# A third buffer for a transposed operand in a fused window-attention training kernel, paid for by loading weights twice

## Chip, cores and metric

The kernel runs on one core of one Trainium2 chip. The metric is the device time of one execution in microseconds; the time before is 1979.6 us, the median of three runs (1979.23 to 1980.32). Single executions of this kernel scatter by up to about 1.5%, and not every chip gives the same median, so each comparison below names the runs of the kernel before that were made beside it on the same chip. Chips are called by the numbers in the records of the runs; that of the first result isn't recorded.

In the text, TensorE does the matrix products, ScalarE is ACT in the profile, VectorE is DVE, GpSimd is POOL, and SyncE is SP, which here does nothing but issue transfers.

## The reference

The forward pass of attention in 8x8 windows of a 256x256 image with 384 channels, and its gradients for the input and for both weight matrices, all in bfloat16:

```python
B, H, W, C = x.shape                     # 1, 256, 256, 384
win = 8
xw  = windows(x)                         # [1024 windows, 64 tokens, C]
qkv = xw @ wqkv
q, k, v = qkv[..., :C], qkv[..., C:2*C], qkv[..., 2*C:]
p = softmax(einsum('bqc,bkc->bqk', q, k) * C**-0.5)
o = einsum('bqk,bkc->bqc', p, v) @ wo
out = image(o)
# reference(x, wqkv, wo, grad_out): out and the vjp's gradients of x, wqkv and wo
```

(The two reshapes between image and windows are abbreviated as `windows` and `image`.)

## The kernel before

The kernel multiplies the weight matrices with each other at the start, so that each window needs only two projections: y from the input (X) and h from the output gradient (DO). It works in 128 steps of 8 windows (512 tokens; the code calls such a unit a quad). Within step n, TensorE does the attention products of quad n, the scores of quad n+2 and the projections of quad n+3. The parts that matter here:

```python
NX, ND, NXT, NDT, NYH, NTOK, NVW = 13, 5, 3, 2, 2, 2, 9
...
YHT = sb.tile([P, NYH, 2, CK, 512], BF16, name="YHT")      # y and h, channels on the partitions
YH = sb.tile([P, NTOK, 2, CK * 4, P], BF16, name="YH")     # the same, tokens on the partitions
w_sb = sb.tile([P, CK, J], BF16, name="w_sb")              # the weights, kept to the end

def load_do(q, n):
    for t in range(4):
        q.dma_start(out=DO[:, (n % ND) * 4 + t, :], in_=img(grad_out, n, t))

def turn_yh(n, a):                                         # a transposing transfer, issued by SyncE
    SP.dma_start_transpose(out=YH[:, n % NTOK, a, :, :],
                           in_=YHT[:, n % NYH, a, :, :].rearrange("p m t -> p (m t)"))

def proj(n, a, banks, engs):
    ...                                                    # TensorE into a PSUM bank, then
            ev(engs[i], YHT[:, n % NYH, a, mo, P * t0:P * t1], o)      # the bank is copied to YHT

def chain3(n):                                             # softmax, last part
    ...
    DVE.tensor_reduce(out=ST[:, 3, :], in_=TM[:], axis=AX.X, op=ALU.add)
    POOL.tensor_tensor(out=UM[:], in0=pb[:, 1], in1=bcast(3), op=ALU.mult)
    POOL.tensor_tensor(out=pb[:, 0], in0=TM[:], in1=UM[:], op=ALU.subtract)

def step(n):
    S, A = n + 2, n + 3
    turn_in(n + 4, 0)                      # transposes of X and of DO, also on SyncE
    turn_in(n + 4, 1)
    md(n)                                  # the step's first matrix products
    ...                                    # attention of n, which reads YH[n % NTOK]
    load_do(SP, n + 5)                     # four loads on SyncE
    turn_yh(S, 0)
    turn_yh(S, 1)                          # writes YH[S % NTOK] from YHT[S % NYH]
    ...
    proj(A, 0, ...)                        # overwrites YHT[A % NYH]
    outs(n, ...)
    proj(A, 1, ...)
```

In one step SyncE thus has eight transfers to issue in a fixed order: two transposes of the inputs, four loads of DO, and the pair of YH transposes, which this document calls the YH pair.

Of the kernel before, what the change touches and what calls it, by code (L numbers as in the profile page):

```python
# [9 lines left out]
ALU = mybir.AluOpType  # L10
AX = mybir.AxisListType
BF16 = mybir.dt.bfloat16
# [4 lines left out]
def kernel(  # L17
# [12 lines left out]
    _, H, W, C = x.shape  # L30
    P = 128
    CK = C // P
    J = 3 * C
    JK = J // P
    NQC = W // 32
    NQ = (H // 16) * NQC
    scale = float(C) ** -0.5
    GQ = 6
    NX, ND, NXT, NDT, NYH, NTOK, NVW = 13, 5, 3, 2, 2, 2, 9

    def cut(q):

        out = []
        while q + GQ <= NQ - 2:
            out.append(tuple(range(q, q + GQ)))
            q += GQ
        if q < NQ - 2:
            out.append(tuple(range(q, NQ - 2)))
        return out + [(q,) for q in range(NQ - 2, NQ)]

    groups = [cut(0), [tuple(range(GQ // 2))] + cut(GQ // 2)]
    PE, DVE, ACT, POOL, SP = nc.tensor, nc.vector, nc.scalar, nc.gpsimd, nc.sync

    sb = ctx.enter_context(tc.tile_pool(name="sb", bufs=1))
    pp = ctx.enter_context(tc.tile_pool(name="pp", bufs=1, space=bass.MemoryType.PSUM))
    PS = pp.tile([P, 8, 512], F32, name="PS")
# [3 lines left out]
    XT = sb.tile([P, NXT, 4 * CK, P], BF16, name="XT")  # L60
# [12 lines left out]
    TM = sb.tile([P, 4, 64], F32, name="TM")  # L73
    UM = sb.tile([P, 4, 64], F32, name="UM")
    ST = sb.tile([P, 4, 4], F32, name="ST")
    ACC = sb.tile([P, 2 * CK, C], F32, name="ACC")
    ident = sb.tile([P, P], BF16, name="ident")
    w_sb = sb.tile([P, CK, J], BF16, name="w_sb")
    A_sb = sb.tile([P, CK, C], BF16, name="A_sb")
    AT_sb = sb.tile([P, CK, C], BF16, name="AT_sb")  # L80
    B_sb = sb.tile([P, CK, C], BF16, name="B_sb")
# [16 lines left out]
    def bcast(col):  # L98
        return ST[:, col, :].unsqueeze(2).to_broadcast([P, 4, 64])
# [10 lines left out]
    def turn_in(n, a):  # L110
        src = (X[:, (n % NX) * 4:(n % NX) * 4 + 4, :] if a == 0 else DO[:, (n % ND) * 4:(n % ND) * 4 + 4, :])
        SP.dma_start_transpose(out=XT[:, n % NXT, :, :] if a == 0 else DOT[:, n % NDT, :, :],
                               in_=src.rearrange("p t c -> p (t c)"))
# [35 lines left out]
    def sd(r, w):  # L149
        return PS[HALF[r], 4, w * 256:w * 256 + 256].rearrange("p (t k) -> p t k", t=4)  # L150
# [11 lines left out]
    def chain3(n):  # L162
        pb = PB[:, n % 2]
        DVE.tensor_reduce(out=ST[:, 1, :], in_=PEX[:], axis=AX.X, op=ALU.add)
        DVE.reciprocal(out=ST[:, 2, :], in_=ST[:, 1, :])
        DVE.tensor_tensor(out=pb[:, 1], in0=PEX[:], in1=bcast(2), op=ALU.mult)  # L166
        for w in range(2):
            DVE.tensor_tensor(out=TM[HALF[w]], in0=sd(1 - w, w), in1=pb[HALF[w], 1], op=ALU.mult)  # L168
        DVE.tensor_reduce(out=ST[:, 3, :], in_=TM[:], axis=AX.X, op=ALU.add)
        POOL.tensor_tensor(out=UM[:], in0=pb[:, 1], in1=bcast(3), op=ALU.mult)  # L170
        POOL.tensor_tensor(out=pb[:, 0], in0=TM[:], in1=UM[:], op=ALU.subtract)

    def turn_p(n):
        bb = PS[:, 7, 256:512].bitcast(BF16)
        for t in range(4):
            for a in range(2):
                for w in range(2):
                    r = slice(64 * w, 64 * w + 64)
                    o = t * P + a * 64
                    PE.transpose(bb[r, o:o + 64], PB[r, n % 2, a, t, :], ident[r, r])  # L180
        DVE.tensor_copy(out=TT[:, n % 2, :, :, :].rearrange("p t a k -> p (t a k)"), in_=bb)
# [98 lines left out]
    class Block:  # L280
# [25 lines left out]
        def add(self, bank):  # L306
            self.banks -= 1
            dst = GF if self.last and self.banks == 0 else ACC
            if self.adds:
# [24 lines left out]
    flat = VW[:].rearrange("p a b c -> p (a b c)")  # L334
    wT = flat[:, 0:JK * C].rearrange("p (j c) -> p j c", j=JK)
    wo_sb = flat[:, JK * C:(JK + CK) * C].rearrange("p (m c) -> p m c", m=CK)
    GF = YHT[:, 0].rearrange("p a m t -> p (a m t)")[:, 0:6 * C].rearrange("p (k c) -> p k c", k=6)
    GFT = YHT[:, 1].rearrange("p a m t -> p (a m t)")[:, 0:6 * C].rearrange("p (k c) -> p k c", k=6)
    bank = [0]
# [12 lines left out]
    def step(n):  # L352
        S, A = n + 2, n + 3
        doS, doA = S < NQ, A < NQ
        early = not todo
        if n + 4 < NQ:
            turn_in(n + 4, 0)
            turn_in(n + 4, 1)

        md(n)  # L360
        if early:
            if doA:
                proj(A, 0, (3, 4, 0, 5), (ACT, ACT, ACT, DVE))
            if n + 1 < NQ:
                turn_p(n + 1)
            attn_vw(n, 0, 0)
            vw_ev(n, 0, 0, ACT)
            attn_vw(n, 1, 2 * 512)
            attn_vw(n, 2, 2 * 512 + 2 * C)
            vw_ev(n, 1, 2 * 512, DVE)  # L370
            vw_ev(n, 2, 2 * 512 + 2 * C, ACT)
            attn_vw(n, 3, 0)
            vw_ev(n, 3, 0, ACT)
            if doS:
                stack(S, 0, 0, 3)
                stack(S, 1, 0, 3)
            if n + 5 < NQ:
                load_x(POOL, n + 5)
        else:
            blk = todo.pop(0)  # L380
            nb = len(blk.tiles)
            i1, i2 = (7, 15) if nb == 4 * GQ else (nb // 2, nb)
            blk.mms((3, 4), 0, i1)
            attn2(n, 0, (ACT, ACT))
            if doS:
                stack(S, 0, 0, 3)
            if n + 1 < NQ:
                turn_p(n + 1)
            if doS:
                stack(S, 1, 0, 3)  # L390
            blk.mms((3, 4), i1, i2)
            blk.add(4)
            if n + 5 < NQ:
                load_x(POOL, n + 5)
            attn2(n, 1, (ACT, DVE))
        ready(n)
        if n + 5 < NQ:
            load_do(SP, n + 5)
        if doS:
            turn_yh(S, 0)  # L400
            turn_yh(S, 1)

        dxs(n, 0)
        dxs(n, 1)
        if not early:
            if doS:
                scores(S)
                chain0(S)
            dxs_ev(n, 0, ACT)
            blk.mms((3,), i2, nb)  # L410
        dxs(n, 3)
        dxs(n, 2)
        if early:
            dxs_ev(n, 0, ACT)
            if doS:
                scores(S)
                chain0(S)
        if doS:
            chain2(S)
        dxs_ev(n, 1, ACT)  # L420
        if doS:
            chain3(S)
        if not early:
            blk.add(3)
        if doA:
            proj(A, int(early), (0, 1, 2), (ACT, ACT, ACT))
        else:
            fill(0, 1, 2)
        outs(n, 0, (5, 6), ACT)
        outs(n, 2, (4, 7) if early else (0, 1), ACT)  # L430
        outs_st(n)
        if not early and doA:
            proj(A, 1, (7, 2, 4, 3), (ACT, ACT, ACT, DVE))
        elif not doA:
            fill(7, 2, 4)
# [4 lines left out]
    with tc.manual_schedule():  # L440
# [68 lines left out]
        proj(2, 1, (6, 7, 0, 4), (ACT, ACT, ACT, ACT))  # L509
        for n in range(NQ):  # L510
            step(n)
            if n == 4:
                for m in range(CK):
                    SP.dma_start_transpose(out=woT_sb[:, :, m * P:(m + 1) * P], in_=wo[m * P:(m + 1) * P, :])
# [7 lines left out]
        def ep(o, lt, rr, dst, eng, sc):  # L522
            for mb in range(CK):
                mm(o, lt(mb), rr(mb), mb == 0, mb == CK - 1)
            if eng is ACT:
                ACT.activation(out=dst, in_=o, func=ACTF.Copy, scale=scale if sc else 1.0)  # L526
            elif sc:
                DVE.tensor_scalar(out=dst, in0=o, scalar1=scale, scalar2=None, op0=ALU.mult)
            else:
                DVE.tensor_copy(out=dst, in_=o)  # L530

        def tr(h):
            for mb in range(CK):
                pt = PS[:, h * CK + mb, :].bitcast(BF16)
                for ma in range(CK):
                    PE.transpose(pt[:, ma * P:(ma + 1) * P], GF[:, h * CK + ma, mb * P:(mb + 1) * P], ident[:])
                ev(DVE if mb % 2 == 0 else ACT, GFT[:, h * CK + mb, :], pt[:, 0:C])
# [3 lines left out]
        cut = lambda ma: slice(ma * P, (ma + 1) * P)  # L541
        tr(0)
        for ma in range(CK):
            ep(PS[:, 6 + ma % 2, 0:C], lambda mb: GF[:, mb, cut(ma)], lambda mb: w_sb[:, mb, C:2 * C],
               dw[:, ma, 0:C], DVE if ma == 1 else ACT, True)
        tr(1)
        for ma in range(CK):
            ep(PS[:, ma, 0:C], lambda mb: GFT[:, mb, cut(ma)], lambda mb: w_sb[:, mb, 0:C],
               dw[:, ma, C:2 * C], DVE if ma == 0 else ACT, True)
        SP.dma_start(out=out_2.rearrange("(m p) j -> p m j", p=P)[:, :, 0:2 * C], in_=dw[:, :, 0:2 * C])  # L550
        for ma in range(CK):
            ep(PS[:, 6 + ma % 2, 0:C], lambda mb: w_sb[:, mb, 2 * C + ma * P:2 * C + (ma + 1) * P],
               lambda mb: GF[:, CK + mb, :], dwo[:, ma, :], DVE if ma == 1 else ACT, False)
        ACT.dma_start(out=out_3.rearrange("(m p) n -> p m n", p=P), in_=dwo[:])
        for ma in range(CK):
# [33 lines left out]
```

## Time and profile before

| | before |
|---|---|
| median of runs | 1979.6 us |
| span of the profiled run | 1983.8 us |
| TensorE busy | 1944.9 us, 98% |
| DMA engines, mean busy share in the middle | 1.18 (packet times, which overlap) |
| clean step of TensorE | 14.87 us |
| mean of 109 steps in the middle | 15.12 us |
| ScalarE's wait for the YH transposes | 60.9 us, 64 times |

The prediction below shows and reads the lines. Three things help to read them. A wait `A <- B` is the idle time of A that ended when B ended, with the total, the number of times and the longest. The chain is the work that ended last, followed backwards, so a wait only costs time to the extent that it, or what follows from it, is on the chain. And a queue of transfers has two times: the one in which the issuing engine is held, and the one until the data has landed.

### The profile page before, as it was taken

How to read it: one execution, taken by the hardware profiler on the slowest of the kernel's cores; microseconds unless marked ns; L12 is line 12 of the kernel's file. 1: busy time of each engine (PE TensorE's matmuls, PEld its weight loads, DVE VectorE, ACT ScalarE, POOL GpSimd, SP SyncE). 2: the span in 40 equal slices, each digit the busy share in tenths (PEclk: the TensorE clock that was granted, in tenths of full speed). 3: DMA queues.
4: the chain of work that ended last, by engine and by line, in shares of the span. 5: the costliest groups of instructions: out<-in, count | busy, mean ns of one | idle time of the engine just before them, and what ended most of it. 6: DMA issues, size and time to landing. Idle time of an engine off the chain costs nothing.

```text
span 1983.8 us, 78482 instructions
## 1 busy us (share of the span) xinstructions
PE 1944.9 (98%) x32789; PEld 1364.7 (69%) x32789; DVE 1254.8 (63%) x2595; ACT 1337.1 (67%) x2204; POOL 1317.0 (66%) x2315
## 2 busy tenths in 40 slices
PE   8899999999999999999999999999999999999999
PEld 5566776677667666767766776676677677666766
DVE  5665666666666666666666666666666666656664
ACT  5766766666666676667666766766776766667664
POOL 4766766666666667667667666666766766667653
PEclk9999999999999999999999999999999999999999
DMA  9999999999999999999999999999999999999992
GB/s 215 208 204 212 219 208 207 216 208 200 212 214 212 210 200 210 216 209 216 216 212 210 222 212 196 222 206 210 207 224 205 211 208 218 205 199 222 217 165 68
DMA packets 972260, 409.24 MB, mean 206 GB/s; under 512 B 855296, under 2 KB 947264, under 8 KB 971904
## 3 DMA queue, kind: packets, MB, share of 16 engines
q1 hardware_dynamic: 871632, 251.17, 83.5%
q0 software_dynamic: 98496, 151.78, 30.0%
q8 instruction: 256, 4.19, 0.9%
q10 hardware_dynamic: 1776, 1.28, 0.2%
q14 instruction: 100, 0.82, 0.1%
HBM read 101.84 MB, written 101.84 MB: 103 GB/s over the span
## 4 chain that ended last, share of the span: by engine, by line
PE 85%; DMA 10%; ACT 2%; DVE 1%; issue 1%; POOL 0%; ACTq 0%; DVEq 0%; POOLq 0%
PE PS L86 84%; DMA YH<-YHT 10%; PE PS L180 1%; ACT YHT L90 1%; DMA out_dram<-OS 0%; ACT VW L90 0%; DMA X<-in_x_dram 0%; DVE TM L168 0%; POOL out_dram L278 0%; DVE SS L156 0%; DVE ST L154 0%; ACT DXS L90 0%; ACT VW L526 0%; ACT OS L90 0%; DVE PB L166 0%
## 5 line engine op out<-in xcount | busy, mean ns | idle before, releaser
L278 POOL DMA_DIRECT2D out_dram<-DXS x1024 | 578.0, 571 | 570.5 <-ACT DXS L90 512.2
L86 PE MATMUL PS<-VW,X 64*64 64x384 bf16 (+1 forms) x8661 | 578.1, 325 | 0.0
L86 PEld LDWEIGHTS <-X 64*64 64x64 bf16 (+1 forms) x14805 | 445.2, 106 | 129.0 <-issue 33.6
L86 PEld LDWEIGHTS <-MD 128*128 128x128 bf16 x3840 | 343.1, 98 | 226.2 <-issue 43.2
L90 ACT CAST YHT<-PS 128x512 bf16<-128x512 f32 (+1 forms) x770 | 392.6, 556 | 91.9 <-DMA YH<-YHT 60.9
L90 ACT CAST VW<-PS 128x768 bf16<-128x768 f32 x384 | 294.2, 800 | 141.1 <-PE PS L86 141.0
L104 POOL DMA_DIRECT2D X<-in_x_dram x508 | 289.3, 581 | 25.3 <-PE PS L86 14.2
L220 POOL DMA_DIRECT2D out_dram<-OS x512 | 277.5, 549 | 26.5 <-issue 10.2
L86 PE MATMUL PS<-AT_sb,MD 128*128 128x384 bf16 (+2 forms) x2304 | 294.3, 273 | 0.5 <-ACT DXS L90 0.4
L92 DVE CAST YHT<-PS 128x256 bf16<-128x256 f32 (+1 forms) x129 | 55.2, 429 | 378.2 <-PE PS L86 369.0
L86 PE MATMUL PS<-B_sb,MD 128*128 128x384 bf16 x1536 | 274.1, 326 | 12.5 <-ACT YHT L90 7.8
L86 PE MATMUL PS<-XT,A_sb 128*128 128x512 bf16 (+1 forms) x1170 | 270.3, 376 | 2.6 <-DVE TM L168 1.9
L86 PE MATMUL PS<-DOT,BT_sb 128*128 128x256 bf16 (+1 forms) x1527 | 270.5, 327 | 0.0
L90 ACT CAST DXS<-PS 128x768 bf16<-128x768 f32 x256 | 204.2, 798 | 85.7 <-PE PS L86 75.9
L92 DVE CAST MD<-PS 128x512 bf16<-128x512 f32 x384 | 241.7, 683 | 10.7 <-PE PS L86 10.3
L90 ACT CAST OS<-PS 128x768 bf16<-128x768 f32 x256 | 202.9, 809 | 51.3 <-PE PS L86 45.1
L86 PEld LDWEIGHTS <-BT_sb 128*128 128x128 bf16 x1527 | 149.1, 98 | 112.5
L90 ACT CAST MD<-PS 128x512 bf16<-128x512 f32 x384 | 201.2, 602 | 28.2 <-PE PS L86 27.8
L86 PE MATMUL PS<-YH,PB 64*64 64x256 bf16 (+2 forms) x3072 | 211.7, 270 | 0.0
L160 ACT ACTIVATE PEX<-SS 128x256 f32<-128x256 f32 x128 | 53.3, 417 | 227.9 <-DVE SS L156 227.9
L86 PEld LDWEIGHTS <-PB 64*64 64x64 bf16 x6144 | 192.6, 107 | 16.4 <-issue 2.5
L86 PEld LDWEIGHTS <-A_sb 128*128 128x128 bf16 x1170 | 109.0, 98 | 110.3 <-issue 3.9
(65 smaller groups left out, 1938.6 us busy)
## 6 DMA issues: line engine op xcount, KB each, us to landing
out_dram<-DXS POOLq DMA_DIRECT2D x1024, 48.0 KB
out_dram<-OS POOLq DMA_DIRECT2D x512, 96.0 KB
X<-in_x_dram POOLq DMA_DIRECT2D x508, 96.0 KB
DO<-in_grad_out_dram SPq DMA_DIRECT2D x504, 96.0 KB, 5.1
YH<-YHT SPq DMA_TRANSPOSE x256, 8.2
XT<-X SPq DMA_TRANSPOSE x126, 7.4
DOT<-DO SPq DMA_TRANSPOSE x126, 8.2
DO<-in_grad_out_dram POOLq DMA_DIRECT2D x8, 96.0 KB
```

Source lines behind the costliest of these rows:

```text
L86: PE.matmul(out, lhsT=lhsT, rhs=rhs, start=start, stop=stop, skip_group_check=True)
L90: ACT.copy(out=out, in_=in_)
L92: DVE.tensor_copy(out=out, in_=in_)
L104: q.dma_start(out=X[:, (n % NX) * 4 + t, :], in_=img(x, n, t))
L160: ACT.activation(out=PEX[:], in_=SS[:], func=ACTF.Exp)
L180: PE.transpose(bb[r, o:o + 64], PB[r, n % 2, a, t, :], ident[r, r])
L220: POOL.dma_start(out=img(out_0, n, t), in_=OS[:, n % 2, t, :])
L278: POOL.dma_start(out=img(out_1, n, t)[8 * w:8 * w + 8], in_=DXS[64 * (1 - w):64 * (1 - w) + 64, n % 2, t, :])
```

## The change

The kernel gets a third slot for YHT, so that a projection's result doesn't have to overwrite data whose transpose may not have ended. The room comes from the weights: they are no longer kept (`w_sb` now lies over a buffer that is used later) but loaded a second time shortly before the end, into a buffer that is then free. Apart from that, two elementwise products at the end of the softmax go from GpSimd to VectorE.

```diff
--- before.py
+++ after.py
@@ -36,7 +36,7 @@
     NQ = (H // 16) * NQC
     scale = float(C) ** -0.5
     GQ = 6
-    NX, ND, NXT, NDT, NYH, NTOK, NVW = 13, 5, 3, 2, 2, 2, 9
+    NX, ND, NXT, NDT, NYH, NTOK, NVW = 13, 5, 3, 2, 3, 2, 9
 
     def cut(q):
 
@@ -75,7 +75,6 @@
     ST = sb.tile([P, 4, 4], F32, name="ST")
     ACC = sb.tile([P, 2 * CK, C], F32, name="ACC")
     ident = sb.tile([P, P], BF16, name="ident")
-    w_sb = sb.tile([P, CK, J], BF16, name="w_sb")
     A_sb = sb.tile([P, CK, C], BF16, name="A_sb")
     AT_sb = sb.tile([P, CK, C], BF16, name="AT_sb")
     B_sb = sb.tile([P, CK, C], BF16, name="B_sb")
@@ -167,8 +166,8 @@
         for w in range(2):
             DVE.tensor_tensor(out=TM[HALF[w]], in0=sd(1 - w, w), in1=pb[HALF[w], 1], op=ALU.mult)
         DVE.tensor_reduce(out=ST[:, 3, :], in_=TM[:], axis=AX.X, op=ALU.add)
-        POOL.tensor_tensor(out=UM[:], in0=pb[:, 1], in1=bcast(3), op=ALU.mult)
-        POOL.tensor_tensor(out=pb[:, 0], in0=TM[:], in1=UM[:], op=ALU.subtract)
+        DVE.tensor_tensor(out=UM[:], in0=pb[:, 1], in1=bcast(3), op=ALU.mult)
+        DVE.tensor_tensor(out=pb[:, 0], in0=TM[:], in1=UM[:], op=ALU.subtract)
 
     def turn_p(n):
         bb = PS[:, 7, 256:512].bitcast(BF16)
@@ -334,6 +333,8 @@
     flat = VW[:].rearrange("p a b c -> p (a b c)")
     wT = flat[:, 0:JK * C].rearrange("p (j c) -> p j c", j=JK)
     wo_sb = flat[:, JK * C:(JK + CK) * C].rearrange("p (m c) -> p m c", m=CK)
+    w_sb = flat[:, (JK + CK) * C:(JK + CK) * C + CK * J].rearrange("p (m j) -> p m j", m=CK)
+    w_end = XT[:].rearrange("p n j k -> p (n j k)")[:, 0:CK * J].rearrange("p (m j) -> p m j", m=CK)
     GF = YHT[:, 0].rearrange("p a m t -> p (a m t)")[:, 0:6 * C].rearrange("p (k c) -> p k c", k=6)
     GFT = YHT[:, 1].rearrange("p a m t -> p (a m t)")[:, 0:6 * C].rearrange("p (k c) -> p k c", k=6)
     bank = [0]
@@ -509,6 +510,8 @@
         proj(2, 1, (6, 7, 0, 4), (ACT, ACT, ACT, ACT))
         for n in range(NQ):
             step(n)
+            if n == NQ - 3:
+                SP.dma_start(out=w_end[:], in_=wqkv.rearrange("(m p) j -> p m j", p=P))
             if n == 4:
                 for m in range(CK):
                     SP.dma_start_transpose(out=woT_sb[:, :, m * P:(m + 1) * P], in_=wo[m * P:(m + 1) * P, :])
@@ -541,15 +544,15 @@
         cut = lambda ma: slice(ma * P, (ma + 1) * P)
         tr(0)
         for ma in range(CK):
-            ep(PS[:, 6 + ma % 2, 0:C], lambda mb: GF[:, mb, cut(ma)], lambda mb: w_sb[:, mb, C:2 * C],
+            ep(PS[:, 6 + ma % 2, 0:C], lambda mb: GF[:, mb, cut(ma)], lambda mb: w_end[:, mb, C:2 * C],
                dw[:, ma, 0:C], DVE if ma == 1 else ACT, True)
         tr(1)
         for ma in range(CK):
-            ep(PS[:, ma, 0:C], lambda mb: GFT[:, mb, cut(ma)], lambda mb: w_sb[:, mb, 0:C],
+            ep(PS[:, ma, 0:C], lambda mb: GFT[:, mb, cut(ma)], lambda mb: w_end[:, mb, 0:C],
                dw[:, ma, C:2 * C], DVE if ma == 0 else ACT, True)
         SP.dma_start(out=out_2.rearrange("(m p) j -> p m j", p=P)[:, :, 0:2 * C], in_=dw[:, :, 0:2 * C])
         for ma in range(CK):
-            ep(PS[:, 6 + ma % 2, 0:C], lambda mb: w_sb[:, mb, 2 * C + ma * P:2 * C + (ma + 1) * P],
+            ep(PS[:, 6 + ma % 2, 0:C], lambda mb: w_end[:, mb, 2 * C + ma * P:2 * C + (ma + 1) * P],
                lambda mb: GF[:, CK + mb, :], dwo[:, ma, :], DVE if ma == 1 else ACT, False)
         ACT.dma_start(out=out_3.rearrange("(m p) n -> p m n", p=P), in_=dwo[:])
         for ma in range(CK):
```

## The prediction

> **What bounds the kernel now.** I read the page's busy table first, then the chain of waits, then the waits summed by pair, then the two tiles that the change touches, and last the synchronising engine's own record, because the chain pointed at it.
>
> ```profile
> PE 1944.9 (98%) x32789; PEld 1364.7 (69%) x32789; DVE 1254.8 (63%) x2595; ACT 1337.1 (67%) x2204; POOL 1317.0 (66%) x2315
> DMA  9999999999999999999999999999999999999992
> PEclk9999999999999999999999999999999999999999
> PE 85%; DMA 10%; ACT 2%; DVE 1%; issue 1%; POOL 0%; ACTq 0%; DVEq 0%; POOLq 0%
> ```
>
> TensorE works 98% of the span at the full clock. At most 1983.8 - 1944.9 = 39 us of visible idle time can be won from it, 2% of the span. But the DMA row is as full as the PE row, and the chain passes through a DMA for a tenth of the span, always YH<-YHT. The chain in order of time shows how long a step of TensorE is when nothing holds it:
>
> ```profile
> 943.83 0.18 PE PS L180 x11
> 944.01 0.01 PE PS L86
> 944.02 0.07 PE PS L180 x4
> 944.08 14.62 PE PS L86 x226
> ...
> 1228.74 10.45 DMA YH<-YHT
> 1239.19 0.02 issue
> ...
> 1239.27 0.59 ACT YHT L90
> ```
>
> One clean step is 14.62 + 0.18 + 0.01 + 0.07 = 14.88 us (14.87 between the starts of most steps). The lower lines are a disturbed one: the transposing transfer of YHT lands at 1239.19, only then may ScalarE overwrite that YHT slot, and TensorE, out of PSUM banks, waits for ScalarE. Summed by pair:
>
> ```profile
> ACT YHT L90 <- DMA YH<-YHT: 60.9, 64, 3.3
> PE PS L86 <- ACT YHT L90: 18.7, 31, 1.9
> POOL UM L170 <- DVE ST L169: 12.5, 2, 6.8
> PEld L180 <- POOL PB L171: 1.2, 1, 1.2
> PE PS L180 <- POOL PB L171: 1.0, 1, 1.0
> ```
>
> This is the wait that a third slot takes away. Its whole cost is more than 18.7 us. The view by windows gives the middle of the run as a whole:
>
> ```profile
> 184.25:1832.74 1648.49, 1631.82 (x27905) 1150.86 (x27904) 1054.31 (x2180) 1128.99 (x1856) 1119.39 (x1963) 1.00 1.18 211
> 120.38:184.25 63.87, 60.48 (x1025) 42.76 (x1024) 38.77 (x80) 40.24 (x68) 45.66 (x79) 1.00 1.17 204
> 1907.00:1940.00 33.00, 33.00 (x537) 23.22 (x536) 19.79 (x41) 18.36 (x30) 16.63 (x31) 1.00 0.60 112
> ```
>
> The first stretch holds 109 steps (218 YH transposes are issued in it, two a step): 15.124 us a step, 0.254 over the clean step, 27.7 us in all. The second holds four steps, 63.87 - 4 x 14.87 = 4.4 us. So 32 us is lost to waits in the steady part: the ceiling of what the slots can return. The third stretch, near the end, shows the DMA load once input loads have stopped (share 0.60, against 1.18).
>
> Now the question is why the transfer is late. The tile view of the transposes' line, first in the middle stretch, then in 1907 to 1932:
>
> ```profile
> L116 SPq EVENT_SEMAPHORE  x327: 17/17/28, 187.4 to 1822.6; - x164
> L116 SPq DMA_TRANSPOSE YH<-YHT x218: 1544/2800/5858, 187.5 to 1822.7; - x109
> DMA to landing us min/median/max: 5.3/8.2/12.7
> ...
> L116 SPq DMA_TRANSPOSE YH<-YHT x4: 1424/1560/1681, 1911.6 to 1928.1; - x4
> DMA to landing us min/median/max: 3.8/5.1/6.0
> ```
>
> The reader is to see two things. In 109 steps no semaphore instruction ahead of these transposes lasted over 28 ns: the queue of SyncE never waits for the other engines, it is always behind. And a transpose holds the queue for 2.8 us under load, 1.56 us without. The other transposes have medians of 2.70 and 2.90 us, the four loads of a step 0.60 us each: 2 x 2.80 + 2.70 + 2.90 + 4 x 0.60 = 13.6 us, and with the small instructions between them a full step. In order of time it issues the YH pair 2.3 us after the start of the next step (913.77 against 911.43), while near the end, without load, it is 4.5 us into its own step. It runs about 12 us late.
>
> **What the Trainium skill says.** "Perfetto Trace Analysis", section "What 'DMA-bound' means", names as one of the kinds a queue whose sequencer track is solid DMA slices. This trace agrees: no pause over 28 ns at that line. The same page, section "DMA Instruction — HWDGE (DVE, Sync)", says that the reported window opens when all semaphores are satisfied; so the 2.8 us are descriptor work[...] and not a wait on an engine, which fits that it falls to 1.56 us near the end. "SBUF — State Buffer", section "Who interferes with whom", says that a two-input tensor operation in SBUF contends only with GpSimd instructions that read SBUF; after the change POOL has no such instruction in the loop. No row before can confirm that. "GPSIMD Engine Reference", section "Elementwise — side-by-side cycle accounting", gives GpSimd about twice the time of VectorE; here it is 625 and 725 ns against 424 ns for a 128x256 multiplication on VectorE, so 1.5 to 1.7.
>
> **The change part by part.**
> (1) Third YHT slot. The evacuation of projection n+3 now overwrites what was transposed a whole step earlier. The next need of the same transfer is TensorE's read of YH. In a clean step the first y cast starts 10.2 us in (906.60 against 896.39), the first h cast 13.9 us in; the first YH matmul 1.8 us into the following step, the h one about 2.2. So y may land 14.87 + 1.8 - 10.2 = 6.5 us later than now, h 14.87 + 2.2 - 13.9 = 3.2 us later. The room is thus about 3 us, not a step: NTOK stays 2, and the queue may only become 3 us later still.
> (2) Products on VectorE: minus (625 + 725) ns x 128 = 173 us of POOL (to about 1144), plus 2 x 0.424 x 128 = 109 us of VectorE (to about 1364, 69%). In a step VectorE is idle 2.99 us ahead of its YHT cast, after these products, so 0.85 us fits. It takes PB out from behind POOL's descriptor work, worth the 1.0 us of the one late wait. In the prologue the copies to HYS follow the products on VectorE and lie on the chain: plus 0.85 us once.
> (3) The weights again: 3 x 128 x 1152 x 2 bytes = 0.885 MB. At the mean 206 GB/s that is 4.3 us, issued after step 125, about 1940, where the DMA share is low and the first reader is at 1973. Nothing on the path. The first load only moves to another place.
> Sum outside the steady part: about +1 us. Inside: between -3 and -32.
>
> **The rivals.**
> A, only slots were missing: the lateness is a scatter of some 2 us that 3 us swallow. For it: most steps are clean, in runs of up to ten; waits come in bursts. Then nearly all goes: -28, 1952 us.
> B, the queue sets the pace: it never waits, and averages 15.12 us a step against 14.87. Then a deeper buffer lets it fall 3 us further behind, once, and the wait comes back as TensorE waiting for YH itself. For it: the 28 ns. Then 1979.6 + 1 - 3 = 1978 us.
> C, in between: the queue in clean steps averages nearer 15.03 (my estimate from the starts of the pair in 68 clean steps, uncertain by 0.12), and disturbed steps make the transfers bunch. Removing most waits then gains (15.12 - 15.03) x 115 = 10 us and the 3 us of room: 1968 us.
> D, VectorE becomes late with the PSUM bank 3 addition and holds the last projection: 0.85 of about 1.5 us of slack. A loss of at most some tenths a step in bad steps; I give it little.
>
> **Range and chances.** I weigh B 0.45, C 0.30, A 0.25: 0.45 x 3 + 0.30 x 13 + 0.25 x 28 = 12 us, less 1 us of the prologue: 1968.5, and I say 1968 us. Eight in ten: 1951 to 1980. Two per cent would be 39.6 us, more than the 32 us that waits take, so faster by over 2% has 0.02; slower by over 2% needs a new wait of 0.3 us in every step, 0.02; within 2% 0.96.
>
> **What would show it.** The pair ScalarE YHT waiting for YH<-YHT must be near zero; if it isn't, the reading of the slots is wrong. If A holds, TensorE's wait total falls by 19 us and nearly all steps are 14.87. If B holds, TensorE or its weight loads wait for the DMA YH<-YHT, a pair that is absent now, and the middle stretch stays near 15.1 a step. SyncE's semaphore instructions stay at 28 ns under B and C. VectorE near 1364 us, POOL near 1144. What would make it wrong: a transpose that holds the queue for another time than 2.8 us because POOL's transfers come at other moments, up or down; 0.2 us on each of four would be 100 us a run up to the floor of TensorE.

## The result

The changed kernel takes 1957.57 us (median of four runs: 1956.62, 1964.61, 1958.46, 1956.68), the kernel before 1979.96 us (median of four: 1979.6, 1979.23, 1980.32, 1988.91). The ratio is 0.9884, with a 95% interval from 0.9848 to 0.9921: 1.2% less time, which is inside 2%. A ratio in this document is the mean time of the one kernel's fast runs over the mean time of the other's fast runs of the same rounds, so it isn't quite the ratio of the medians quoted. Executions over 1.5% slower than the fastest of the same kernel are left out of the means.

The page of the changed kernel, busy times, DMA row and chain:

```profile
PE 1934.0 (99%) x32789; PEld 1350.2 (69%) x32789; DVE 1362.9 (70%) x2851; ACT 1352.0 (69%) x2204; POOL 1135.4 (58%) x2059
DMA  9999999999999999999999999999999999999992
PE 97%; DVE 1%; ACT 1%; issue 0%; DMA 0%; ACTq 0%; DVEq 0%
```

TensorE now makes up 97% of the chain (it was 85%), and the DMA, 10% before, has gone from it. Yet the DMA row is as full as it was. TensorE's waits, summed by pair (from the longest down):

```profile
PE PS L85 <- DVE TM L167: 4.3, 5, 1.8
...
PE PS L85 <- ACT YHT L89: 0.3, 1, 0.3
```

The line numbers are one lower than before, because a line was removed above; L85 is the L86 of before. The wait for ScalarE's YHT has fallen from 18.7 us to 0.3, and ScalarE's own wait for YH<-YHT, 60.9 us before, is not in the list any more. In its place there is nothing: TensorE doesn't wait for YH itself either. The windows view of the middle, 109 steps, and of four early steps (columns as in the prediction's lines of this view: window, length, busy time of PE, PEld, DVE, ACT and POOL, clock, DMA share, GB/s):

```profile
180.68:1803.67 1622.99, 1622.22 (x27905) 1137.48 (x27904) 1146.80 (x2398) 1142.13 (x1855) 966.15 (x1747) 1.00 1.18 214
121.19:180.68 59.49, 59.49 (x1025) 41.73 (x1025) 42.17 (x88) 41.99 (x70) 37.67 (x68) 1.00 1.17 216
```

1622.99 / 109 = 14.89 us a step, against 15.12 before, and 59.49 / 4 = 14.87 against 15.97. Both stretches are TensorE without a gap, and the DMA engines, at the same share, moved 214 GB/s in place of 211. The chain in order of time has TensorE alone for whole steps on end; one with a rare gap of 0.35 us, the largest exception in the 60 us that I read:

```profile
928.04 7.27 PE PS L85 x102
935.31 0.35 issue
935.66 7.51 PE PS L85 x124
```

I also took the start of every step from the trace. Over steps 6 to 124 the profiled run of before spends 31.9 us more than 119 clean steps would take, that of after 2.1 us. That difference, 29.8 us, is the whole of the difference between the two spans (29.1 us), less the 0.8 us that after loses before step 6 begins. The profiled run of before was one of its longer runs, so by the medians the gain is 22.4 us.

The moved products, as groups of the page by form, first before, then after:

```profile
L171 POOL TENSOR_TENSOR PB<-TM,UM 128x256 bf16<-128x256 f32 x128 | 93.2, 728 | 10.0
L170 POOL TENSOR_TENSOR UM<-PB,ST 128x256 f32<-128x256 bf16 x128 | 80.2, 627 | 14.5 <-DVE ST L169 12.5
```

```profile
L170 DVE TENSOR_TENSOR PB<-TM,UM 128x256 bf16<-128x256 f32 x128 | 54.4, 425 | 4.4
L169 DVE TENSOR_TENSOR UM<-PB,ST 128x256 f32<-128x256 bf16 x128 | 54.3, 424 | 4.4
```

And the queue of SyncE. First the timeline of before over one round of its eight transfers (start, time held, what), then that of after:

```profile
898.93 6.06 SPq L116 DMA_TRANSPOSE YH<-YHT  x2
905.21 2.74 SPq L112 DMA_TRANSPOSE XT<-X  x1
908.17 2.90 SPq L112 DMA_TRANSPOSE DOT<-DO  x1
911.13 2.54 SPq L108 DMA_DIRECT2D DO<-in_grad_out_dram  x4
913.77 6.88 SPq L116 DMA_TRANSPOSE YH<-YHT  x2
```

```profile
1166.90 5.26 SPq L115 DMA_TRANSPOSE YH<-YHT  x2
1172.39 2.32 SPq L111 DMA_TRANSPOSE XT<-X  x1
1174.93 2.46 SPq L111 DMA_TRANSPOSE DOT<-DO  x1
1177.44 3.02 SPq L107 DMA_DIRECT2D DO<-in_grad_out_dram  x4
1180.57 6.05 SPq L115 DMA_TRANSPOSE YH<-YHT  x2
```

In both kernels a row ends where the next begins, but for 0.05 to 0.25 us: the queue is without a pause, in after too. Over all steps, its transfer instructions hold it for 14.0 us of a step in the median in both kernels (the middle half of the steps lies between 13.9 and 14.2), and the rest is small instructions; the pauses of over 0.15 us add up to 4.9 us over the middle steps, in each of the two. (The view of SyncE's own waits doesn't show this: it lists 625.4 us of waits for TensorE ahead of L112 before, and 606.3 us at the same line after.) Its pace, from one YH pair to the same pair a step later, averages 15.12 us over the middle steps before, and 14.86 us after. That is the surprise: the queue that "sets the pace" is without a pause in both kernels, and runs faster in the one with a third slot.

### The profile page after: what moved, and what is told of

The parts are those of the page before. It is cut to its first block, busy times and chain, and to the rows that moved or that the text cites. A ratio compares the mean times of both kernels' runs of the same rounds, so it can differ in the third digit from the quotient of the medians.

```text
span 1954.7 us, 78332 instructions
## 1 busy us (share of the span) xinstructions
PE 1934.0 (99%) x32789; PEld 1350.2 (69%) x32789; DVE 1362.9 (70%) x2851; ACT 1352.0 (69%) x2204; POOL 1135.4 (58%) x2059
## 2 busy tenths in 40 slices
DMA packets 972659, 410.12 MB, mean 210 GB/s; under 512 B 855312, under 2 KB 947280, under 8 KB 972304
## 4 chain that ended last, share of the span: by engine, by line
PE 97%; DVE 1%; ACT 1%; issue 0%; DMA 0%; ACTq 0%; DVEq 0%
PE PS L85 95%; PE PS L179 2%; ACT VW L89 0%; DVE TM L167 0%; DMA X<-in_x_dram 0%; ACT YHT L89 0%; DVE SS L155 0%; DVE ST L153 0%; ACT DXS L89 0%; ACT VW L529 0%; ACT OS L89 0%; DVE PB L165 0%; DVE ST L163 0%; PE PS L187 0%; ACTq L103 0%
## 5 line engine op out<-in xcount | busy, mean ns | idle before, releaser
L85 PE MATMUL PS<-VW,X 64*64 64x384 bf16 (+1 forms) x8661 | 574.6, 324 | 0.0
L85 PEld LDWEIGHTS <-X 64*64 64x64 bf16 (+1 forms) x14805 | 435.1, 106 | 121.0 <-issue 22.6
L85 PEld LDWEIGHTS <-MD 128*128 128x128 bf16 x3840 | 343.3, 98 | 215.5 <-issue 31.7
L89 ACT CAST YHT<-PS 128x512 bf16<-128x512 f32 (+1 forms) x770 | 409.2, 553 | 16.5 <-PE PS L85 6.8
L103 POOL DMA_DIRECT2D X<-in_x_dram x508 | 281.7, 565 | 48.9 <-PE PS L85 36.5
L85 PE MATMUL PS<-AT_sb,MD 128*128 128x384 bf16 (+2 forms) x2304 | 294.3, 273 | 1.0 <-issue 0.6
L85 PE MATMUL PS<-B_sb,MD 128*128 128x384 bf16 x1536 | 271.5, 326 | 4.2 <-ACT DXS L89 2.1
L85 PE MATMUL PS<-XT,A_sb 128*128 128x512 bf16 (+1 forms) x1170 | 270.4, 376 | 3.3 <-DVE TM L167 1.8
L85 PE MATMUL PS<-DOT,BT_sb 128*128 128x256 bf16 (+1 forms) x1527 | 270.5, 327 | 0.0
L85 PEld LDWEIGHTS <-BT_sb 128*128 128x128 bf16 x1527 | 149.1, 98 | 112.5
L85 PE MATMUL PS<-YH,PB 64*64 64x256 bf16 (+2 forms) x3072 | 210.4, 269 | 0.0
L85 PEld LDWEIGHTS <-PB 64*64 64x64 bf16 x6144 | 187.3, 107 | 19.6 <-issue 2.5
L85 PEld LDWEIGHTS <-A_sb 128*128 128x128 bf16 x1170 | 109.0, 98 | 111.0 <-issue 4.8
```

The source lines that it names most:

```text
L85: PE.matmul(out, lhsT=lhsT, rhs=rhs, start=start, stop=stop, skip_group_check=True)
L89: ACT.copy(out=out, in_=in_)
L103: q.dma_start(out=X[:, (n % NX) * 4 + t, :], in_=img(x, n, t))
```

## The experiments

One measure is used throughout: the **lateness** of the queue in step n is the start of the YH pair that is issued in the code of step n, less the start of that step on TensorE. I worked it out from the trace for each step. Medians are over steps 10 to 118.

How late may it be? The pair's first transfer lands about 8 us after its start, the second, which starts some 2.8 us later, about 11 us after (from the medians of before, in the prediction). With two slots the copy of the next y into the same slot wants to begin 10.2 us into the next step, the copy of h 13.9 us in. So waits begin at a lateness of about 14.87 + 10.2 - 8.2 = 16.9 us for y and 14.87 + 13.9 - 11.0 = 17.8 us for h. With three slots the next need is TensorE's reading of YH, two steps on: 29.74 + 1.8 - 8.2 = 23.3 us for y, and 29.74 + 2.2 - 11.0 = 20.9 us for h. The third slot moves the limit from about 17 to about 21 us. These are estimates from medians, and single transfers scatter around them. Before had a median lateness of 17.3 us, at its limit; after 17.0 us, with a range of 13.6 to 20.4, just inside its own.

The theories, by the letters that the expectations use: **S**, slots: the queue has room to keep TensorE's pace, and only the two slots turned its scatter into waits. **Q**, queue: the queue's own pace is over 14.87 us a step, so what the third slot gives is given once and the wait comes back. **P**, products: the gain comes from the products that left GpSimd.

The first four experiments ran together on chip 3, where before took 1983.45 us (median of seven runs, 1973.4 to 1987.52).

### Only the slots

```diff
 # kernel after
-        DVE.tensor_tensor(out=UM[:], in0=pb[:, 1], in1=bcast(3), op=ALU.mult)
-        DVE.tensor_tensor(out=pb[:, 0], in0=TM[:], in1=UM[:], op=ALU.subtract)
+        POOL.tensor_tensor(out=UM[:], in0=pb[:, 1], in1=bcast(3), op=ALU.mult)
+        POOL.tensor_tensor(out=pb[:, 0], in0=TM[:], in1=UM[:], op=ALU.subtract)
```

> The third YHT slot and the reload, the products left on POOL. Theory S (the slots took away the waits): ScalarE's wait for YH<-YHT near zero, 1957 to 1961 us, the 1.0 us of a late PB at most on top. Theory P (the products off POOL made the transfers quicker, the slots only help): TensorE still loses several us, now at the PB transposes or at YH, 1968 us or more. Theory Q (the transfer queue sets the pace): about 1976 us.

Measured: median 1957.5 us (1954.46, 1956.97, 1958.02, 1972.9), ratio 0.9901 (0.9842 to 0.9959). Steps 6 to 124 cost 3.9 us over the clean steps, ScalarE's wait for YH is gone, and a first trace of the next limit appears among TensorE's waits, at a lateness of up to 22.6 us:

```profile
PE PS L85 <- DMA YH<-YHT: 1.8, 3, 1.3
```

The slots carry the gain (with the reload that makes room for them, and the other layout of the memory that it brings). P is false.

### Only the products

```diff
 # kernel before
-        POOL.tensor_tensor(out=UM[:], in0=pb[:, 1], in1=bcast(3), op=ALU.mult)
-        POOL.tensor_tensor(out=pb[:, 0], in0=TM[:], in1=UM[:], op=ALU.subtract)
+        DVE.tensor_tensor(out=UM[:], in0=pb[:, 1], in1=bcast(3), op=ALU.mult)
+        DVE.tensor_tensor(out=pb[:, 0], in0=TM[:], in1=UM[:], op=ALU.subtract)
```

> Two slots as before, the two products on VectorE. Theory S: 1979 to 1981 us, waits of ScalarE for YH<-YHT near 61 us as before, and 1 us gained at PB and lost in the prologue. Theory P: half or more of the gain is here, 1970 us or less, and that wait falls under 30 us.

Measured: median 1977.92 us (1973.5 to 1983.77), ratio 0.9986 (0.9949 to 1.0023): no effect that these runs can tell from zero. The waits of the old kind are there, in the profiled run (its fastest) somewhat fewer than before:

```profile
ACT YHT L90 <- DMA YH<-YHT: 45.1, 52, 3.0
...
PE PS L86 <- ACT YHT L90: 10.7, 20, 1.5
```

### What makes the queue late: moving three transposes

In step 4 the kernel transposes wo by three transfers on the same queue, which are needed only at the end. The lateness jumps there. If the queue had no speed to spare, one delay would never be made up, so I moved these three transfers to the end, in before and in after.

```diff
 # kernel before, and in a second run kernel after
-            if n == 4:
+            if n == NQ - 3:
                 for m in range(CK):
                     SP.dma_start_transpose(out=woT_sb[:, :, m * P:(m + 1) * P], in_=wo[m * P:(m + 1) * P, :])
```

> The kernel before with one edit: the three transposes of wo, which the SyncE queue issues after step 4, are issued after step 125. Before, the queue's lateness jumps from 9 to 17 us at that place and stays. If the queue can keep TensorE's pace (theory S), its lateness stays near 9 us of the step for the whole run, two slots suffice, the wait for YH<-YHT is near zero and the time is 1952 to 1960 us without any third slot. If the queue is slower than TensorE by itself (theory Q, 15.03 to 15.12 us a step against 14.87), its lateness grows by 0.16 to 0.25 us a step and reaches 17 us after 32 to 50 steps; then the waits come as before: 1966 to 1974 us.

Measured: median 1977.44 us (1968.14 to 1982.79), ratio 0.9976 (0.9934 to 1.0018). In the profiled run ScalarE waits for YH<-YHT 67 times, 56.4 us in all, nearly as before. The timeline of SyncE's queue shows the start of the pairs from step 4 on:

```profile
102.12 5.90 SPq L116 DMA_TRANSPOSE YH<-YHT  x2
...
132.84 5.46 SPq L116 DMA_TRANSPOSE YH<-YHT  x2
...
211.15 7.12 SPq L116 DMA_TRANSPOSE YH<-YHT  x2
```

Seven steps lie between 102.12 and 211.15: 15.6 us a step. The lateness of steps 4, 6, 8, 10, 12 and 14 was 8.4, 12.9, 13.0, 16.1, 17.5 and 19.0 us. So both theories missed. Without the jump the lateness doesn't stay at 9 us, as S had it, and it doesn't creep up by some tenths a step, as Q had it: it climbs by about 1.1 us a step until it is at 17, and there it stays, in this kernel held by the waits. Part of the climb is TensorE's: its steps 4 and 5 take 13.09 us each, 3.6 us less than two clean steps, and the climb from step 4 to step 12 is 9.1 us. Against 14.87 us a step the queue loses 0.7 us. So the queue has no fixed pace: 15.6 us a step here, 15.15 over the middle steps of the same run. Nor does every run climb: in the one with the slots only, the lateness lies between 13.9 and 15.6 us in steps 6 to 19.

> The changed kernel with the transposes of wo issued after step 125 as well. Theory S: no wait is left for it to take away but the two long weight-load gaps around steps 3 and 4 (0.8 us in all): 1955 to 1957 us, and the lateness of the queue is near 9 us where it can keep it, near 17 where it drifts by itself. Theory Q: the lateness drifts up to about 17 us within 50 steps.

Measured: median 1975.57 us of 1959.55, 1968.44, 1982.69 and 1993.77 (a slow run), ratio 0.9945 (0.9881 to 1.0009). The spread is too wide for a verdict on the time. The profiled run is a fast one, 1957.7 us of span with 3.6 us over the clean steps; its lateness climbed to 17.2 us within ten steps, as in the experiment above.

### Pace against lateness

This made me sort the steps of the traces by lateness and take the mean pace of the queue to the next pair (mean, with its standard error, in us a step):

| lateness | before | after |
|---|---|---|
| under 16 us | 16.07 ± 0.34 | 15.29 ± 0.17 |
| 16 to 17 us | 15.52 ± 0.18 | 14.95 ± 0.18 |
| 17 to 18 us | 14.96 ± 0.10 | 14.66 ± 0.17 |
| over 18 us | 14.63 ± 0.16 | 14.47 ± 0.14 |

In these two profiles, the later the queue is, the faster it goes on. Some of this is only chance, since a step that is late by scatter tends to be followed by one nearer to the mean. In after the lateness had no drift over 108 steps though nothing held it.

But the rule doesn't hold for all profiles. Those of the three-slot kernels on chip 1, reported below, don't repeat it: beyond 18 us the mean pace is 14.91 ± 0.10 us in the one and 15.14 ± 0.11 in the other. Over the five profiles of kernels with three slots and unchanged traffic in the loop (steps 6 to 117), it is 15.24 us at 16 to 17 us of lateness, 14.53 at 18 to 20, and 15.13 again beyond 20. And lateness doesn't explain the difference between the two kernels: after is the faster one in every row of the table. With the number of steps that before has in the four rows (7, 30, 47 and 24), after's paces would average 14.74 us, not 15.12. So why the same transfers, without a pause, take 15.12 us a step in the one kernel and 14.86 in the other is not shown.

### Fewer transfers on the SyncE queue

If the issuing were the limit, taking four of its eight transfers away should give the queue a lot of room. These runs, the one with more bytes and one with a slower TensorE were made together on chip 13, where before took 1986.99 us (median of seven, 1980.77 to 2003.12).

```diff
 # kernel after
-            load_do(SP, n + 5)
+            load_do(POOL, n + 5)
```

> The changed kernel, with the four loads of grad_out of each step issued by POOL and not by SyncE: 2.4 us of issuing less a step on the queue that is late. If the limit of that queue is its own issuing, it catches up: its lateness falls from about 17 us towards the 4.5 us where its data are ready, and its semaphore instructions begin to wait; the time stays 1954 to 1958 us, with less spread. If the limit is the transfers themselves (the same bytes on the same engines), the lateness stays within 2 us of 17 less 2.4 and nothing waits.

Measured: 2134.11 us (2121.71 to 2146.63), ratio 1.0718 (1.0643 to 1.0793). Both forecasts missed by far. TensorE now waits for YH itself, 110 us in all, and is slower as well: busy for 1987.5 us against 1934.0, at a mean granted clock of 0.982 against 1.000 in after. Whether the lower clock follows from the waits is not tested.

```profile
PE PS L85 <- DMA YH<-YHT: 110.2, 72, 4.4
```

The SyncE queue, in its timeline, got pauses, here of 1012.68 - (999.19 + 7.30) = 6.2 us ahead of the transpose of X:

```profile
999.19 7.30 SPq L115 DMA_TRANSPOSE YH<-YHT  x2
1012.68 1.50 SPq L111 DMA_TRANSPOSE XT<-X  x1
```

The pause ends with a load of X, which landed at 1012.54 us. GpSimd had become the late one: in the median it issues the X loads of a step 24.9 us after the step's start, against 1.3 us in after, and the queue of SyncE waits for them (worked out from the two traces, steps 10 to 117). So this run moved the limit to another queue, and doesn't say what SyncE's queue would do with less to issue.

The packets took longer in all as well. The queues of the page, after and then this run (packets, MB, share of 16 engines' span):

```profile
q1 hardware_dynamic: 872032, 252.05, 83.8%
q0 software_dynamic: 98496, 151.78, 30.0%
```

```profile
q1 hardware_dynamic: 801184, 203.65, 71.6%
q0 software_dynamic: 122112, 200.18, 41.2%
```

48 MB went from the first queue to the second, with about the same total, 410 MB. The two shares add up to 1.138 of 1954.7 us and 1.128 of 2131.3 us: 2224 and 2404 us of packet time, 8% more for the same bytes. The Trainium skill, "DMA: Bandwidth & Descriptors", section "Issuing engines are not separate DMA queues", says that a second initiating engine saves only the sequencer's time for the start. Here the kernel, 1% faster than before without this edit, is 7% slower than before with it. Which part of the loss is GpSimd's lateness, which slower packets and which the clock isn't settled by this run.

The same with two slots (before with the products on VectorE, and this edit):

> Two slots, products on VectorE, and the loads of grad_out issued by POOL. If lateness alone makes the waits and issuing makes the lateness: no wait for YH<-YHT, 1953 to 1958 us, as good as a third slot. If the transfers themselves set the lateness: the pair lands about 2.4 us sooner at best, the waits fall by half, 1962 to 1972 us.

Measured: 2180.94 us (2176.24 to 2185.04), ratio 1.0952 (1.089 to 1.1014):

```profile
ACT YHT L90 <- DMA YH<-YHT: 274.4, 148, 4.8
...
PE PS L86 <- ACT YHT L90: 166.3, 123, 3.3
```

With transfers this late the third slot is worth 2180.94 - 2134.11 = 47 us, and it doesn't make the wait go away: with three slots it shows up at YH. This is what the prediction's rival B had described, in a kernel whose transfers really come too late.

### More bytes

```diff
 # kernel after
+    DUM = sb.tile([P, C], BF16, name="DUM")
...
             load_do(SP, n + 5)
+            SP.dma_start(out=DUM[:], in_=img(x, n, 0))
```

> The changed kernel plus one more load of 96 KB a step on the SyncE queue, never read: 3% more bytes and 0.6 us more issuing a step. If transfers were saturated at TensorE's pace (theory Q in its milder form, capacity just 14.87 us a step), each step becomes 0.3 to 0.5 us longer once the room of 3 us is used up: 1990 us or more, with TensorE waiting for YH. If the queue gets quicker when it is late (theory S as the lateness of about 17 us in all runs suggests), the lateness rises by a us or so and the time stays under 1965 us.

Measured: 2056.52 us (2050.91 to 2065.16), ratio 1.0319 (1.0246 to 1.0392). One more load of 96 KB a step, 422.22 MB in place of 410.12 MB (3%), makes a step 15.78 us long on average, 0.9 us more than after's 14.89 in its first profile. (TensorE's busy time is 1963.4 us against 1934.0, at a mean granted clock of 0.993; that is about 0.2 us of the 0.9.) The lateness goes to a median of 24.7 us, beyond the limit of three slots, and TensorE waits for YH; the waits, and then the windows view, whose DMA rate is 208 GB/s against after's 214:

```profile
PE PS L86 <- DMA YH<-YHT: 76.0, 71, 2.6
```

```profile
184.00:1832.00 1648.00, 1581.09 (x26791) 1098.60 (x26793) 1098.12 (x2301) 1100.91 (x1780) 927.88 (x1676) 0.99 1.17 208
```

So S in its strong form is false: the queue has no room at TensorE's pace, and one load more, some 0.6 us of issuing, costs 0.9 us in every step. The edit adds bytes and issuing together, so which of them counts isn't separated.

### Slower TensorE

The other way round: the first of each three products of the output is issued twice (the second writes the same values), four matrix products of about 0.16 us more a step; the result stays right.

```diff
 # kernel after, and in a second run kernel before
-                mm(PS[:, bb[i], 0:C], MD[:, m, t0 + i, 2:4, :].rearrange("p a k -> p (a k)"), B_sb[:, m, :],
-                   m == CK - 1, m == 0)
+                for _ in range(2 if m == CK - 1 else 1):
+                    mm(PS[:, bb[i], 0:C], MD[:, m, t0 + i, 2:4, :].rearrange("p a k -> p (a k)"), B_sb[:, m, :],
+                       m == CK - 1, m == 0)
```

> The changed kernel with 4 of the output matmuls of a step issued twice, 0.65 us more TensorE a step, the result unchanged. If the queue has a pace of its own of 14.87 to 15.1 us a step, it gains 0.4 us or more in each step of 15.5 us, reaches its data (4.5 us) after some 30 steps and waits there. If its pace follows its place in TensorE's step, its lateness settles at some value well above 4.5 and stays, at 15.5 us a step, with no wait of its own. Time 1957 + 128 x 0.65 = 2040 us in both.

Measured in a single run, so of unknown state: 2067.93 us. A clean step is now 15.52 us, the mean 15.71 over steps 10 to 118. The lateness fell to a median of 6.0 us, and in many steps it is exactly 6.0: the queue is ahead and is held by the other engines. So its own pace is below 15.52 us a step. The mean exceeds the clean step by 0.19 us, some 23 us over the run; most of that are gaps of TensorE that the profile puts down to nothing ("issue"), and I have no cause for them:

```profile
PE PS L85 <- issue: 20.8, 20, 2.4
```

This run also tests a piece of evidence. The queue waits here, ahead of the transposes of the inputs and of the loads of DO, and yet the semaphore instructions ahead of those transposes last no longer than the 28 ns of before; what shows the waiting is the pauses in its timeline:

```profile
L111 SPq EVENT_SEMAPHORE  x633: 17/28/28, 184.8 to 1828.3; - x159
```

```profile
1166.97 1.44 SPq L111 DMA_TRANSPOSE XT<-X  x1
1170.51 1.42 SPq L111 DMA_TRANSPOSE DOT<-DO  x1
1172.95 3.37 SPq L107 DMA_DIRECT2D DO<-in_grad_out_dram  x4
```

From 1168.41, the end of the first row, to 1170.51 no transfer is issued, from 1171.93 to 1172.95 neither. Over all steps the transfers hold the queue for 12.5 us of 15.5 in the median, in a quarter of them for 11.3 or less. So short semaphore instructions don't show that a queue never waits. A long one, though, does show a wait: near the end of before, where the prediction left this line out, one ahead of the YH pair lasts 11.5 us.

```profile
L116 SPq EVENT_SEMAPHORE  x6: 17/28/11508, 1907.0 to 1928.0; - x6
```

With two slots, on chip 1 (before: median 1988.77 us of eleven runs, 1972.09 to 2002.43):

> The kernel before, two slots, with 4 output matmuls of a step issued twice (0.65 us more TensorE a step). The queue and TensorE are within 0.2 us a step of each other before; if so, at 15.52 us a step the queue catches up, its lateness falls to about 6 us of the step, and two slots are enough: ScalarE's wait for YH<-YHT under 5 us, and a time within 0.5% of the 2068 us of the changed kernel with the same edit. If the queue's pace before is its own 15.12 us with wide scatter, some waits stay.

Measured in a single run of unknown state: 2054.99 us. ScalarE doesn't wait for YH<-YHT at all, and the lateness has a median of 6.0 us too. With a TensorE that is 4% slower, two slots are enough. (That this run is 0.6% faster than the one with three slots is across two chips, and that one had more of the gaps without a cause; I draw nothing from it.)

### Fewer bytes

Also on chip 1, before with only three of the four DO tiles loaded in the loop. The result is wrong (relative error 0.70), since a quarter of DO is stale.

```diff
 # kernel before
-    def load_do(q, n):
-        for t in range(4):
+    def load_do(q, n, nt=4):
+        for t in range(nt):
...
-            load_do(SP, n + 5)
+            load_do(SP, n + 5, 3)
```

> The kernel before, two slots, with three instead of four loads of grad_out a step (the result is wrong on purpose): 3% fewer bytes and 0.6 us less issuing. If queue and TensorE are neck and neck, this little tips it: lateness well under 17 us, ScalarE's wait for YH<-YHT under 10 us in place of 61, 1950 to 1957 us with two slots. If the waits come from bursts that have nothing to do with the mean load, at least 30 us of that wait stay and the time is over 1965 us.

Measured: fast runs of 1955.83, 1956.61 and 1957.78 us, ratio 0.9845 (0.9802 to 0.9887). The profiled run was a slow one (1986.81 us) and isn't used, so whether the waits are gone in the fast ones isn't seen. With 3% fewer bytes, and one transfer less to issue, which this edit doesn't separate, two slots are as fast as three were in the first result, and faster than three on this chip (1978.15 us, below). Together with the previous experiments this brackets the balance: 3% of traffic one way or 4% of TensorE time decide whether slots matter.

### After once more, and a variant

Again on chip 1: after unchanged, and after with other PSUM banks for the outputs of the early steps, which wait for VectorE's TM in the first lines of the waits.

> The changed kernel once more, unchanged, on the chip of the next three runs: the measure for them. 0.985 to 0.992 of the kernel before if the gain holds on another chip.

Measured: 1978.15 us, median of six (1969.69, 1976.32, 1976.7, 1979.61, 1984.25, and a slow 2003.39), ratio 0.9948 (0.9911 to 0.9985). The same change brought 0.5% here and 1.2% in the first result. The profiled run has 15.3 us over the clean steps, a median lateness of 18.5 us with a maximum of 25.4, and the wait at the new limit:

```profile
PE PS L85 <- DMA YH<-YHT: 7.8, 9, 2.4
```

The variant:

```diff
 # kernel after
-        outs(n, 0, (5, 6), ACT)
-        outs(n, 2, (4, 7) if early else (0, 1), ACT)
+        outs(n, 0, (3, 5) if early else (5, 6), ACT)
+        outs(n, 2, (6, 7) if early else (0, 1), ACT)
```

> The changed kernel with other PSUM banks for the output products of the first three steps, which have no block of weight gradients to fill in: (3, 5) and (6, 7) in place of (5, 6) and (4, 7). It takes away TensorE's waits of 0.71 us for ScalarE's DXS and 0.68 us for VectorE's TM in each of steps 0 to 2: 3 x 1.39 = 4.2 us less, 0.2%, unless the first product of the next step then waits for bank 6 (0.5 us each). Below the spread of some runs; the profile should show the two pairs gone.

Measured: 1973.49 us, median of six (1962.87 to 1987.66), ratio 0.9924 (0.9875 to 0.9973). The first three steps take 12.41, 14.02 and 14.02 us in place of 13.73, 14.68 and 14.68, 2.6 us less, of which step 3 gives back 1.3. But the profiled run lost more to the transfers than this gained:

```profile
PE PS L85 <- DMA YH<-YHT: 19.9, 18, 1.9
```

The ratio is the best of the correct kernels on this chip, but its interval covers that of the unchanged kernel, so it isn't shown to be better.

## Why the prediction was right, and where it was off

The time, 1957.57 us, lies in the range from 1951 to 1980 and in the class that had been given 0.96. That alone says little, since the range holds the forecasts of all three rivals A, B and C (1952, 1978 and 1968 us). The gain is 22.4 us where 11.6 were forecast, so the steps deserve a look one by one.

**The wait and its ceiling: right.** The pair ScalarE YHT waiting for YH<-YHT went from 60.9 us to nothing. The ceiling of 32 us in the steady part was a good measure: 31.9 us by the starts of the steps, of which 29.8 were won in the profiled runs.

**The chances of the rivals: the step that was off.** The prediction gave most weight, 0.45, to B, "the queue sets the pace", and 0.25 to A. In the first result A's size came: nearly all went, 22 to 29 us. B's term of the sum, 3 us, and C's, 13, were both too small. The step that failed is B's reading of 15.12 us as the queue's own pace, from which it followed that "the wait comes back as TensorE waiting for YH itself". In after the pace was 14.86 us over the middle steps, TensorE waited 0.3 us for ScalarE's YHT, and not at all for YH. The 15.12 had been measured with the wait in it: two parts that are coupled through their buffers have one mean pace, which says nothing on which of them sets it. How the wait makes the queue of before slower, though that queue shows no pause, is not shown.

**A's reason is not shown.** A had a scatter that 3 us swallow. In after the lateness does stay between 13.6 and 20.4 us, which fits. But the queue has no stock of spare speed: with 3% more bytes the wait that B foretold is there, 76 us of it, and on chip 1, where before was 9 us slower as well, it is there in part with the unchanged kernel. Where lateness starts low it climbed in two runs, so it is not scatter about a fixed pace, and the sorted steps of the profiles on chip 1 speak against the simple rule that a late queue is a faster one. What sets the queue's pace stays open, and no run here changes the moment of the transfers while leaving all else. Also open is how much of the difference between the first result and chip 1 belongs to the chip and how much to the hour.

**The evidence of 28 ns: too narrow.** The prediction read from the short semaphore instructions that the queue never waits. The claim was true for the middle of before (its timeline is without a pause), but the evidence doesn't carry it, as the slower TensorE shows: 28 ns there too, with pauses of 2 us between the transfers. The skill's "What 'DMA-bound' means" asks for a solid track of slices, which is the better reading, but not proof that the queue is the limit: the track of after is as solid, and TensorE makes up 97% of its chain.

**The room of a third slot: right.** About 3 us was worked out, and the waits at YH do appear where the lateness goes over 21 us (22.6 in the run with the slots only, 25.4 on chip 1), and not where it stays under (20.4 in after).

**The products: right in size, and worth nothing.** VectorE rose by 108.1 us to 1362.9 (forecast 1364), GpSimd fell by 181.6 to 1135.4 (forecast 1144). The wait for PB is gone. The run with the slots only is as fast, so this part gains nothing that shows. Nor did D come: VectorE's added time holds nothing up.

**The start: right in sum, not in place.** The forecast was 0.85 us once. Step 0 begins only 0.17 us later (36.83 against 36.65 us), as the copies to HYS behind the products take 0.95 us on the chain in place of 1.36. But step 6 begins 0.81 us later (121.19 against 120.38): steps 3 and 4 have become longer, by 0.51 and 0.34 us, and steps 0 to 2 shorter by 0.07 us each. That the sum agrees is luck.

**The reload: right.** It is issued at 1900.80 us, holds the queue for 0.9 us, and steps 125 to 127 take 18.78, 14.52 and 28.55 us, before 18.78, 14.52 and 28.58. In the trace no instruction waits for it.

## What to carry to other kernels

When two parts run in lockstep, their common pace is not evidence for either; slow one of them down, or give one a few per cent more or less to do, and see which one the time follows. One more buffer is worth what it is worth only near the balance: here two slots showed no wait with a slower TensorE and were as fast as three with less traffic, the third gave 22 us at the balance, and 47 us of a loss of nearly 200 where transfers came late. And a transfer queue's waiting is to be read from the pauses in its timeline and from where in the step its transfers start, not from the length of the instructions ahead of them alone. A queue without a pause is not yet shown to be the limit.

## What the Trainium skill lacked or had wrong

- No page says that a queue which never pauses can run at different paces with the same transfers per step: 15.6 us a step over seven steps of the run with the transposes of wo moved, 15.12 over the middle of before, 14.86 over that of after. The runs don't show why.
- "Perfetto Trace Analysis", section "DMA Instruction — HWDGE (DVE, Sync)", has the window of a transfer open once all semaphores are satisfied, and the slower TensorE agrees: the queue paused for 2.1 us ahead of a transfer, outside every window. What the page lacks is that a wait can also lie inside the window of the semaphore instruction ahead of a transfer: 11.5 us at the end of before, at most 28 ns in the run with the slower TensorE.
- "DMA: Bandwidth & Descriptors", section "Issuing engines are not separate DMA queues", says what a second initiating engine saves, and not what it can cost. Moving four loads a step from SyncE to GpSimd made GpSimd issue its own X loads 24.9 us into a step in place of 1.3, and turned a ratio to before of 0.9884 to 0.9948 into 1.0718 with three slots (1.0952 with two), with 8% more packet time for the same bytes.
- No page says how far a kernel at such a balance moves from one set of runs to the next: the kernel before had medians of 1980.0, 1983.5, 1987.0 and 1988.8 us in four of them (chips 3, 13 and 1, the first not recorded), and the same change gave ratios of 0.9884 and 0.9948.
